# A normalisation's sums over four channel groups: one instruction with a single input in place of a chain of additions

## The chip, the core and the metric

The kernel runs on one core of one Trainium2 chip. The core's engines run side by side and wait for one another through semaphores: TensorE (PE in the profile, its weight loads PEld) multiplies matrices into PSUM, VectorE (DVE) and GpSimd (POOL) do elementwise work and sums along a partition, ScalarE (ACT) does functions of one input, and SyncE (SP) issues most DMAs. Data lie in SBUF, 128 partitions wide; matmul results lie in PSUM, which DVE and ACT can read. The metric is the device time of one execution in microseconds; the kernel's time is the median of its runs.

## What is computed

Eight batches of 576 positions with 512 channels, in float32. Linear attention in eight heads gives x; a gated convolution mixer gives a second x; then a Fourier mixing, a normalisation over the channels and a two-layer network with a residual:

```python
X = np.fft.fft(np.fft.fft(x, axis=1), axis=2)
u = x + np.real(X).astype(np.float32)
mu = np.mean(u, axis=-1, keepdims=True)
var = np.mean((u - mu) ** 2, axis=-1, keepdims=True)
un = (u - mu) / np.sqrt(var + 1e-06)
out = u + np.maximum(un @ w_ch1, 0.0) @ w_ch2        # 512 -> 2048 -> 512
```

The change concerns the two means over the 512 channels.

## The kernel before

The kernel has four stages: attention with the conversion of the weights (to about 360 us of the span), the mixer and the Fourier transforms of batches 0 to 5 (to about 600 us), the last two batches together with the normalisation of the first block (to about 655 us), and the two-layer network (the rest).

The network works on nine blocks of 512 positions (`TB`; `NBK` = 9 of them), each as two halves of 256 columns (`HB`). The channels lie on partitions: 512 channels are four groups of 128, so a block's activations are the tile `A`, 128 partitions x 4 groups x 512 columns. There are two passes over the blocks (`blocks`): the first with one half of the hidden units, blocks 0 to 8 upwards; the second with the other half, blocks 8 to 0 downwards. The first pass normalises each block and stores it to DRAM (`un_scr`); the second loads the stored blocks again. Products are done in three matmuls with operands split into a high and a low part (`o_hi` on ACT, `o_lo` on DVE or POOL), and a block's 2 x 2 products are replaced by seven (`prep_un` makes the seven left operands `un`, `c1_units` the first layer with its ReLU and the operands `h` of the second, `c2_units` the second layer, whose results are added into four accumulators `acc`). Each of a block's two groups of hidden units takes fourteen such products, of twelve matmuls each.

`ln_stages` is the normalisation of one block. For each half it adds the four channel groups of `A` into `s1` (three additions of 256 columns), splits `s1` into `sh` and `sl` and has PE sum over the partitions with a matrix of 1/512 (two matmuls into `mean`). DVE subtracts `mean` from `A`. ACT squares `A` into the tiles `T0` (groups 0 and 1) and `T1` (groups 2 and 3), and three more additions of 256 columns add these four groups into `s1`. Again `sh`, `sl` and a matmul; ACT takes the root, DVE the reciprocal (two of 128 columns a half) and multiplies `A` by it. `T0` and `T1` serve `prep_un` afterwards.

The order of all this is not written out. Each step is noted in `ops` with the engines that may do it, a time for each, and the tiles that it reads and writes. `place_ops` then takes one step after the other: each engine gets, among the steps that are ready, the one due first, and a step with two engines to choose from (`"vp"`: DVE or POOL) goes to POOL if POOL would have it done before DVE. The additions are such steps (`e1` is `"vp"`), as are the `sl`, `un`, `h` and differences of `c`. The planner's times for a step are `COST`, and 0.87 us for a reciprocal; they know nothing of one engine holding up another. Tiles named `wo` and `wg` in rows below are spare parts of weight tiles that serve as `h`. All instructions of one helper carry one line: L647 is every `o_tt`, L72 a low part on DVE, L75 one on POOL, L66 a high part, L650 every `o_act`, L806 a product of the first layer, L875 one of the second, L721 and L722 the means.

Of the kernel before, what the change touches and what calls it, by code (L numbers as in the profile page):

```python
# [7 lines left out]
F32 = mybir.dt.float32  # L8
# [4 lines left out]
ALU = mybir.AluOpType  # L13
AX = mybir.AxisListType
# [10 lines left out]
HB = TB // 2  # L25
# [9 lines left out]
def attention_moe_mixer_kernel(  # L35
# [18 lines left out]
    nc = tc.nc  # L54
    mm = nc.tensor.matmul

    def pool(stack, name, bufs, space=None, side=None):
        kw = {} if space is None else {"space": space}
        if side is not None:
            kw["side"] = side  # L60
        if space is not DRAM:
            kw["reuse_waits"] = "tile"
        return stack.enter_context(tc.tile_pool(name=name, bufs=bufs, **kw))
# [521 lines left out]
    tl = {}  # L585
    ops = []

    def w_tiles(p, i, j):
        return [[p.tile([128, 7, 128], F32R, name=f"w{i}_{j}_{o}_{k}") for k in range(2)] for o in range(2)]

    def w_views(t):
        return [t[:, 896 * k:896 * k + 896].rearrange("p (q f) -> p q f", f=128) for k in range(2)]

    def open_mlp():
        p = pool(lx, "lx", 1, side=R)
        P["pss"] = pool(lx, "pss", 1, PSUM, side=R)
        wt[0].append(w_tiles(p, 0, 0))
        tl["s1"] = p.tile([128, TB], F32, name="s1")
        tl["A"] = p.tile([128, 4, TB], F32, name="A")
        for n in ("sh", "sl"):  # L600
            tl[n] = p.tile([128, HB], F32R, name=n)
        for i in range(2):
            tl["T", i] = p.tile([128, 2, HB], F32, name=f"T{i}")
            wr.append(p.tile([128, 7, 128], F32, name=f"wr{i}"))
        tl["mean"] = P["pss"].tile([128, HB], F32, name="mean")
        for i in range(7):
            un_op.append([p.tile([128, 2, HB], F32R, name=f"un{i}_{k}") for k in range(2)])
        wt[0].append(w_tiles(p, 0, 1))
        g = [P["g1"].tile([128, 2304], F32R, tag=f"g{i}", name=f"wg{i}") for i in range(2)]
        wt[0].append([w_views(t) for t in g])  # L610
        wt[0].append([w_views(wo_all[:, i]) for i in range(2)])
        h_more.extend(t[:, 1792:2304].rearrange("p (o f) -> p o f", f=HB) for t in g)
        h_more.append(wo_all[:, :, 1792:2048])
# [19 lines left out]
    def op(e, cols, fn, reads, writes, dur=None, more=0.0):  # L633
        if dur is None:
            dur = {k: COST[k][0] + COST[k][1] * cols / 1000 for k in e}
        else:
            dur = {e: dur}
        ops.append((dur, fn, reads, writes, more))

    def o_hi(dst, src, cols, r, w):  # L640
        op("a", cols, lambda e: hi_act(dst, src), r, w)

    def o_lo(e, dst, src, hi, cols, r, w):
        op(e, cols, lambda e: (lo_dve if e == "v" else lo_pool)(dst, src, hi), r, w)

    def o_tt(e, o, x, y, alu, cols, r, w):
        op(e, cols, lambda e: (nc.vector if e == "v" else nc.gpsimd).tensor_tensor(out=o, in0=x, in1=y, op=alu), r, w)  # L647

    def o_act(o, x, func, cols, r, w, **kw):
        op("a", cols, lambda e: nc.scalar.activation(out=o, in_=x, func=func, **kw), r, w)  # L650
# [57 lines left out]
    def ln_stages(t, e1=K["ln"]):  # L708
        a, s1 = tl["A"], tl["s1"]
        halves = [slice(0, HB), slice(HB, TB)]  # L710

        def add(o, x, y, e, r, w):
            o_tt(e, o, x, y, ALU.add, HB, r, w)

        def mean(k):
            sh, sl, p = tl["sh"], tl["sl"], tl["mean"]
            o_hi(sh, s1[:, halves[k]], HB, [("s1", k)], ["sh"])
            o_lo(e1, sl, s1[:, halves[k]], sh, HB, [("s1", k), "sh"], ["sl"])

            def f(e):  # L720
                mm(p, ones, sh, start=True, stop=False)  # L721
                mm(p, ones, sl, start=False, stop=True)  # L722
            op("m", 0, f, ["sh", "sl"], ["mean"], 0.218)
            return p

        for k, hk in enumerate(halves):
            for c in range(1, 4):
                add(s1[:, hk], s1[:, hk] if c > 1 else a[:, 0, hk], a[:, c, hk], e1,
                    [("A", c // 2, k), ("A", 0, k), ("s1", k)], [("s1", k)])
        for k, hk in enumerate(halves):  # L730
            p = mean(k)
            for c in range(2):
                b = a[:, 2 * c:2 * c + 2, hk]
                o_tt("v", b, b, p.unsqueeze(1).to_broadcast([128, 2, HB]), ALU.subtract, 2 * HB,
                     ["mean", ("A", c, k)], [("A", c, k)])
        for k, hk in enumerate(halves):
            for c in range(2):
                q = tl["T", c]
                o_act(q, a[:, 2 * c:2 * c + 2, hk], ACTF.Square, 2 * HB, [("A", c, k)], [("T", c)])
                if c:  # L740
                    add(s1[:, hk], s1[:, hk], q[:, 0], e1, [("s1", k), ("T", c)], [("s1", k)])
                    add(s1[:, hk], s1[:, hk], q[:, 1], e1, [("s1", k), ("T", c)], [("s1", k)])
                else:
                    add(s1[:, hk], q[:, 0], q[:, 1], e1, [("T", c)], [("s1", k)])
        for k, hk in enumerate(halves):
            p = mean(k)
            o_act(s1[:, hk], p, ACTF.Sqrt, HB, ["mean"], [("s1", k)], bias=eps)
        for k, hk in enumerate(halves):
            for z in range(2):
                x = s1[:, k * HB + z * 128:k * HB + z * 128 + 128]  # L750
                op("v", 0, lambda e, x=x: nc.vector.reciprocal(out=x, in_=x), [("s1", k)], [("s1", k)], 0.87)  # L751
            for c in range(2):
                b = a[:, 2 * c:2 * c + 2, hk]
                o_tt("v", b, b, s1[:, hk].unsqueeze(1).to_broadcast([128, 2, HB]), ALU.mult, 2 * HB,
                     [("s1", k), ("A", c, k)], [("A", c, k)])
        if t:
            store_un(t)

    def store_un(t):
        o_dma([(un_scr[t], tl["A"])], AK, [("un_scr", t)], 1024, K["sq"] if t == 0 else "d")  # L760
# [240 lines left out]
    def run_last(b):  # L1001
        ps = [P["ps"].tile([128, 512], F32, tag="ps", name=f"ps{i}") for i in range(4)]
        ps += [P["ps2"].tile([128, 512], F32, tag="ps2", name=f"ps{i}") for i in (4, 5)]
        ring = ((("ps", i % 6), ps[i % 6]) for i in range(1000))
        tl["fs"] = P["fs"].tile([128, 2, NE], F32, tag="fs", name="fs")
        tl["eo"] = P["x2"].tile([128, 2, 4, NE], F32, tag="eo", name="eo")
        tl["u"] = P["x2"].tile([128, 4, S], F32, tag="u", name="u")
        tl["u256"] = P["x2"].tile([97, S], F32, tag="u256", name="u256")
        y = [P["x2"].tile([128, 2, 2, NL], F32R, tag=f"Y{i}", name="Y") for i in range(2)]
        xb = P["x2b"].tile([128, 4, 2, NE], F32, tag="x2", name="x2")  # L1010
        f = fhl[b]
        load_a(0, u_scr)
        drain(prep_w(0, 0, K["w0"]))
        drain(prep_w(0, 1, K["w0"]))
        ln_stages(0, K["ln0"])
        note_FD(b, f, y, ring)
        note_W(b + 1, geo[b + 1], xb, f, ring)
        note_SD(b, x2[b], y, ring)
        if K["wl"]:
            drain(prep_w(0, 2, K["w"]))  # L1020
        note_FD(b + 1, f, y, ring)
        note_SD(b + 1, xb, y, ring)
        prep_un(0, K["un0"])
        op("m", 0, lambda e: None, [("un", i, k) for i in range(7) for k in range(2)]
           + [("w", 0, j, o, k) for j in range(2) for o in range(2) for k in range(2)], [], 0.0)
        with tc.manual_schedule():
            for i, e in place_ops():
                ops[i][1](e)
        ops.clear()
# [339 lines left out]
```

## Time and profile before

| | us |
|---|---|
| median of 3 runs (1435.16 to 1440.01) | 1435.16 |
| the profiled execution | 1437.34 |
| its span in the profile | 1435.5 |
| from 677 to 1022 us: first pass of the network | 345 |
| one block of the first pass, 890.45 to 934.52 | 44.07 |
| one block of the second pass, 1105 to 1145 | 40.00 |

The profile page gives busy time by engine; further views of the same trace give it by stretch, or list the instructions of one engine in order of time, each with its start, its duration and, in brackets, how long the engine was idle before and what ended that. An instruction's duration may overlap the next one's by some 0.08 us on DVE, so a step on a busy engine is read from one start to the next. A duration includes the time in which an instruction that had started could not go on. The chain of waits follows the work that ended last backwards; its pieces do not overlap, and "issue" in it is time in which the engine waited for nothing that the profile shows.

### The profile page before, as it was taken

The numbers are of one execution on the slowest core, as the hardware profiler recorded it, in microseconds if no ns is written. First come the engines' busy times: TensorE is split into PE (matmuls) and PEld (weight loads), VectorE is DVE, ScalarE is ACT, GpSimd is POOL, SyncE is SP. The second block draws the span as 40 slices with busy tenths as digits, with TensorE's granted clock in tenths as the row PEclk, the third lists the DMA queues.
The fourth block names the chain that finished last, engine by engine and source line by source line (L and its number), as shares of the span: only waits on it lengthen the run. The fifth ranks groups of instructions, "written<-read, shape, count | busy, mean of one in ns | idle before, by whom it ended". The sixth has DMA issues, their size and how long they took to land.

```text
span 1435.5 us, 35040 instructions
## 1 busy us (share of the span) xinstructions
PE 1347.1 (94%) x14672; PEld 1297.1 (90%) x14672; DVE 1242.7 (87%) x1938; ACT 814.7 (57%) x1513; POOL 706.0 (49%) x526
## 2 busy tenths in 40 slices
PE   6899999997999999986899899999999999999998
PEld 6788888886999999976799899999999999999998
DVE  6689989876899999797999999999899887788876
ACT  5778888764545545464555554555465555444442
POOL 3858887732667666563555555545425111111111
PEclk9899999999999999998999999999999999999999
DMA  6347777741334433336323232222332222222211
GB/s 244 137 182 256 273 266 278 245 169 41 133 133 144 144 134 107 109 109 212 121 82 118 90 111 82 96 97 89 123 124 97 89 74 78 71 89 89 89 40 50
DMA packets 89851, 186.98 MB, mean 130 GB/s; under 512 B 10455, under 2 KB 37335, under 8 KB 87518
## 3 DMA queue, kind: packets, MB, share of 16 engines
q1 hardware_dynamic: 88488, 181.33, 37.2%
q10 hardware_dynamic: 1206, 3.41, 0.6%
q8 instruction: 115, 1.88, 0.5%
q14 instruction: 42, 0.34, 0.1%
HBM read 121.79 MB, written 62.93 MB: 129 GB/s over the span
## 4 chain that ended last, share of the span: by engine, by line
PE 43%; DVE 30%; POOL 9%; issue 8%; ACT 5%; DMA 4%; SPq 0%; ACTq 0%; DVEq 0%; POOLq 0%
PE cx L875 9%; PE x L806 9%; PE cy L875 5%; PE y L806 4%; DVE acc L424 4%; DVE A L647 3%; DVE c L647 3%; PE z L806 3%; PE kv L243 2%; DVE acc L647 2%; PE cz L875 2%; DMA raw<-in_w_ch_dram 2%; DVE s L751 2%; PE nm L282 2%; PE pj L204 2%
## 5 line engine op out<-in xcount | busy, mean ns | idle before, releaser
L875 PE MATMUL cx<-h,w 128*128 128x256 f32 x1152 | 176.2, 286 | 4.8 <-ACT h L66 2.5
L875 PEld LDWEIGHTS cx<-h,w 128*128 128x128 f32 x1152 | 158.3, 194 | 6.7 <-ACT h L66 3.1
L66 ACT ACTIVATE h<-c 128x512 fp32r<-128x512 f32 x180 | 111.6, 627 | 38.6 <-DVE c L647 22.2
L647 POOL TENSOR_TENSOR c<-c,c 128x512 f32<-128x512 f32 x35 | 49.7, 1421 | 167.9 <-ACT h L650 128.2
L647 DVE TENSOR_TENSOR acc<-cx,acc 128x512 f32<-128x512 f32 x144 | 98.1, 681 | 32.9 <-PE cx L875 32.2
L650 ACT ACTIVATE c<-c 128x512 f32<-128x512 f32 x108 | 67.9, 630 | 100.6 <-DVE c L647 99.3
L806 PE MATMUL x<-un,w 128*128 128x256 f32 x864 | 117.0, 285 | 7.6 <-DVE eo L647 6.9
L875 PE MATMUL cy<-h,w 128*128 128x256 f32 x864 | 117.3, 284 | 4.6 <-DVE h L72 1.9
L75 POOL TENSOR_TENSOR h<-c,h 128x512 fp32r<-128x512 f32 x33 | 48.1, 1459 | 148.9 <-ACT h L66 148.7
L806 PEld LDWEIGHTS x<-un,w 128*128 128x128 f32 x864 | 109.9, 193 | 8.2 <-issue 7.1
L424 DVE SCALAR_TENSOR_TENSOR acc<-xf,cw,acc 128x576 f32<-128x576 f32 x128 | 105.0, 820 | 11.9 <-ACT acc L422 10.6
L875 PEld LDWEIGHTS cy<-h,w 128*128 128x128 f32 x864 | 108.9, 191 | 7.0 <-DVE h L72 2.5
L243 PE MATMUL kv<-vraw,ke 128*64 128x66 f32 x2560 | 97.6, 230 | 14.6 <-ACT ke L222 9.8
L243 PEld LDWEIGHTS kv<-vraw,ke 128*64 128x64 f32 x2560 | 85.1, 141 | 26.2 <-ACT ke L222 13.2
L72 DVE TENSOR_TENSOR h<-c,h 128x512 fp32r<-128x512 f32 x111 | 104.2, 940 | 1.3 <-ACT h L66 0.7
L211 DVE TENSOR_REDUCE m<-pj 128x8 f32<-128x1024 f32 (+1 forms) x80 | 88.7, 1108 | 10.6 <-PE pj L204 10.6
L204 PE MATMUL pj<-wp,kqraw 64*128 64x128 f32 x1152 | 89.4, 294 | 5.7 <-DMA kqraw<-in_k_dram 4.9
L204 PEld LDWEIGHTS pj<-wp,kqraw 64*128 64x128 f32 x1152 | 73.8, 194 | 19.6 <-issue 18.1
L214 DVE TENSOR_TENSOR y<-pj,m 128x1024 f32<-128x1024 f32 (+1 forms) x80 | 88.7, 1109 | 0.4
L282 PE MATMUL nm<-kvT,qe 128*64 128x65 f32 x2304 | 84.4, 225 | 2.8 <-issue 1.3
L75 POOL TENSOR_TENSOR ge<-gs,ge 128x580 fp32r<-128x580 f32 x32 | 46.7, 1460 | 76.1 <-ACT ge L66 76.1
L99 POOL TENSOR_SCALAR mt<-mt 128x1024 f32<-128x1024 f32 (+1 forms) x21 | 55.6, 2650 | 57.4 <-DVE mt L97 47.3
(249 smaller groups left out, 4222.4 us busy)
## 6 DMA issues: line engine op xcount, KB each, us to landing
raw<-in_w_ch_dram SPq DMA_DIRECT2D x16, 1024.0 KB, 8.2
wr<-w_scr SPq DMA_DIRECT2D x32, 448.0 KB, 3.4
vraw<-in_v_dram SPq DMA_DIRECT2D x16, 660.0 KB, 9.3
x_scr<-xT SPq DMA_DIRECT2D x32, 288.0 KB, 6.5
xf<-x_scr SPq DMA_DIRECT2D x8, 1152.0 KB, 5.9
out_dram<-acc SPq DMA_DIRECT2D x36, 256.0 KB, 2.2
kqraw<-in_k_dram SPq DMA_DIRECT2D x15, 576.0 KB, 8.3
kqraw<-in_q_dram SPq DMA_DIRECT2D x15, 576.0 KB, 7.4
```

What stands on the lines that cost most here:

```text
L66: nc.scalar.activation(out=dst, in_=src, func=ACTF.Copy)
L72: nc.vector.tensor_tensor(out=dst, in0=src, in1=f32(hi), op=ALU.subtract)
L75: nc.gpsimd.tensor_tensor(out=dst, in0=src, in1=f32(hi), op=ALU.subtract)
L204: mm(p[:, h, o:o + F], t[r, w, 128 * c:128 * c + 128], wp[r, :], start=True, stop=True)
L211: nc.vector.tensor_reduce(out=m, in_=pv, axis=AX.X, op=ALU.max, apply_absolute_value=True)
L214: nc.vector.tensor_tensor(out=y, in0=pv, in1=m.unsqueeze(3).to_broadcast([128, 2, 2 * n, F]), op=ALU.subtract)
L243: mm(t[p, w, :], e[:, a, h, j, p], tv[:, h, slot, :], start=slot % 5 == 0 and w == 0, stop=slot % 5 == 4 and w == 3, skip_group_check=True)
L282: mm(t[p, 2 * j + h, 0:65], e[:, a, h, j, p], kt[:, 2 * h + a, b, :], start=(a == 0), stop=(a == 1))
L424: nc.vector.scalar_tensor_tensor(out=acc, in0=shifted(t), scalar=cw[:, m, t:t + 1], in1=acc, op0=ALU.mult, op1=ALU.add)
L647: op(e, cols, lambda e: (nc.vector if e == "v" else nc.gpsimd).tensor_tensor(out=o, in0=x, in1=y, op=alu), r, w)
L806: mm(p[:, n], l, v[:, kt], start=first and n + kt + m == 0, stop=kt == 1 and m == 2, skip_group_check=True)
L875: mm(p[:, o], v, r[:, n], start=first and o + n + m == 0, stop=n + m == 3, skip_group_check=True)
```

## The change

Each chain of three additions becomes one `tensor_reduce` on DVE: it reads a view of the four channel groups with the group as the innermost index, so four elements that are 512 columns (2 KB, in `A`) or 256 columns (1 KB, in `T`) apart, adds them and writes one. For the second sum the two tiles `T0` and `T1` become the halves of one tile `T`. The steps no longer have POOL to choose; the planner counts 1.1 us for each.

```diff
+        tl["T"] = p.tile([128, 2, 2, HB], F32, name="T")
         for i in range(2):
-            tl["T", i] = p.tile([128, 2, HB], F32, name=f"T{i}")
+            tl["T", i] = tl["T"][:, i]
...
-        def add(o, x, y, e, r, w):
-            o_tt(e, o, x, y, ALU.add, HB, r, w)
-
...
+        def total(k, v, r):
+            o = s1[:, halves[k]]
+            op("v", 0, lambda e: nc.vector.tensor_reduce(out=o, in_=v, axis=AX.X, op=ALU.add), r, [("s1", k)], 1.1)
+
         for k, hk in enumerate(halves):
-            for c in range(1, 4):
-                add(s1[:, hk], s1[:, hk] if c > 1 else a[:, 0, hk], a[:, c, hk], e1,
-                    [("A", c // 2, k), ("A", 0, k), ("s1", k)], [("s1", k)])
+            total(k, a[:, :, hk].rearrange("p c s -> p s c"), [("A", 0, k), ("A", 1, k)])
...
             for c in range(2):
                 q = tl["T", c]
                 o_act(q, a[:, 2 * c:2 * c + 2, hk], ACTF.Square, 2 * HB, [("A", c, k)], [("T", c)])
-                if c:
-                    add(s1[:, hk], s1[:, hk], q[:, 0], e1, [("s1", k), ("T", c)], [("s1", k)])
-                    add(s1[:, hk], s1[:, hk], q[:, 1], e1, [("s1", k), ("T", c)], [("s1", k)])
-                else:
-                    add(s1[:, hk], q[:, 0], q[:, 1], e1, [("T", c)], [("s1", k)])
+            total(k, tl["T"].rearrange("p c o s -> p s (c o)"), [("T", 0), ("T", 1)])
```

Since the planner places every step anew, the order changes around the sums too. On DVE, in a block in the middle of the first pass, the rows from the mean's subtraction to the last sum of squares stood like this before (`s_9173` is `s1`, `T_9177` and `T_9179` are `T0` and `T1`, `c` and `h` belong to the first layer, `acc` to the second):

```order
L647 TENSOR_TENSOR A<-A,mean 128x2x256 x2
L647 TENSOR_TENSOR c_9638<-y,c_9638 128x512
L647 TENSOR_TENSOR s_9173<-T_9177 128x256
L647 TENSOR_TENSOR acc_9679<-cx,acc_9679 128x512
L647 TENSOR_TENSOR c_9637<-c_9638,c_9637 128x512
L647 TENSOR_TENSOR A<-A,mean 128x2x256 x2
L850 SCALAR_TENSOR_TENSOR h_1_9659<-x_9643,h_0_9658 128x512
L647 TENSOR_TENSOR s_9173<-T_9177 128x256
L72 TENSOR_TENSOR h_1_9653<-c_9637,h_0_9652 128x512
L647 TENSOR_TENSOR s_9173<-s_9173,T_9179 128x256
L647 TENSOR_TENSOR c_9639<-c_9639,c_9637 128x512
L647 TENSOR_TENSOR s_9173<-s_9173,T_9179 128x256
```

With the change the same stretch of DVE, from the sums of `A` on, is this:

```order
L726 TENSOR_REDUCE s_9173<-A 128x256 x2
L72 TENSOR_TENSOR sl<-s_9173,sh 128x256
L648 TENSOR_TENSOR c_9630<-x_9634,c_9630 128x512
L648 TENSOR_TENSOR acc_9671<-cx,acc_9671 128x512
L648 TENSOR_TENSOR acc_9669<-cy,acc_9669 128x512
L648 TENSOR_TENSOR A<-A,mean 128x2x256 x2
L72 TENSOR_TENSOR sl<-s_9173,sh 128x256
L648 TENSOR_TENSOR acc_9670<-cx,acc_9670 128x512
L726 TENSOR_REDUCE s_9173<-T 128x256
L648 TENSOR_TENSOR A<-A,mean 128x2x256 x2
L648 TENSOR_TENSOR c_9629<-y,c_9629 128x512
L846 SCALAR_TENSOR_TENSOR h_1_9646<-x_9634,h_0_9645 128x512
```

One more reduction of `T` stands right behind it. The chain of adds between rows of `h` and `c` is gone, and the differences of `c` and one `h` have left this stretch for POOL. POOL had this before, in the rows from the first layer's last `h` to the low part of the second mean:

```order
L75 TENSOR_TENSOR wo<-c_9638,h_0_9660 128x2x256
L647 TENSOR_TENSOR s_9173<-A 128x256
L647 TENSOR_TENSOR s_9173<-s_9173,A 128x256
L75 TENSOR_TENSOR h_1_9651<-c_9637,h_0_9650 128x512
L75 TENSOR_TENSOR sl<-s_9173,sh 128x256
L647 TENSOR_TENSOR s_9173<-s_9173,T_9179 128x256 x2
L647 TENSOR_TENSOR c_9638<-c_9639,c_9638 128x512
L75 TENSOR_TENSOR sl<-s_9173,sh 128x256
```

With the change POOL has this there:

```order
L75 TENSOR_TENSOR wo<-c_9629,h_0_9651 128x2x256
L75 TENSOR_TENSOR un_1_9188<-T,un_0_9187 128x512
L75 TENSOR_TENSOR h_1_9642<-c_9628,h_0_9641 128x512
L75 TENSOR_TENSOR h_1_9648<-c_9630,h_0_9647 128x512
L75 TENSOR_TENSOR sl<-s_9173,sh 128x256
L648 TENSOR_TENSOR c_9628<-c_9629,c_9628 128x512
L648 TENSOR_TENSOR c_9629<-c_9630,c_9629 128x512
```

POOL's four adds of a block and two of its three `sl` are gone; it has one more each of `h`, of the first and of the second step of `T` in `prep_un`, two more differences of `c`, and one less each of `un` and `wo`. On DVE a block has eight adds less and four reductions more, two `sl`, one `un` and one `wo` more, and one step of each kind of `T`, two differences of `c` and one `h` less.

## Rows read from the trace of the kernel before

**Rows 1.** The page: busy us of each engine, share of the span, instructions.
```profile
PE 1347.1 (94%) x14672; PEld 1297.1 (90%) x14672; DVE 1242.7 (87%) x1938; ACT 814.7 (57%) x1513; POOL 706.0 (49%) x526
```

**Rows 2.** Stretch, length; busy PE, PEld, DVE, ACT, POOL (x instructions); clock, DMA share, GB/s.
```profile
604.00:677.00 73.00, 54.95 (x378) 52.07 (x376) 62.63 (x94) 42.16 (x84) 35.32 (x21) 0.91 0.49 166
677.00:1022.00 345.00, 323.18 (x2589) 315.91 (x2590) 334.00 (x474) 184.03 (x332) 193.88 (x146) 0.99 0.30 97
```

**Rows 3.** The same view, one block of each pass.
```profile
890.45:934.52 44.07, 42.34 (x344) 41.36 (x345) 42.65 (x62) 23.68 (x44) 23.90 (x19) 1.00 0.29 96
1105.00:1145.00 40.00, 40.00 (x337) 40.00 (x337) 34.28 (x50) 19.83 (x34) 7.31 (x6) 1.00 0.25 80
```

**Rows 4.** Chain of waits in that block: start, length, what.
```profile
899.31 0.13 PE mean L722
...
933.87 0.61 DVE h L72
...
934.52 1.57 PE cx L875 x11
```

**Rows 5.** DVE's timeline there: start, duration, line, operation, tiles, sizes, idle before.
```profile
904.84 0.42 DVE L647 TENSOR_TENSOR s<-T 128x256 f32<-128x256 f32 x1
905.18 1.23 DVE L72 TENSOR_TENSOR h<-c,h 128x512 fp32r<-128x512 f32 x1
906.33 1.51 DVE L647 TENSOR_TENSOR s<-s,T 128x256 f32<-128x256 f32 x1
...
909.30 0.94 DVE L751 RECIPROCAL s<-s 128x128 f32<-128x128 f32 x1
910.16 0.62 DVE L72 TENSOR_TENSOR h<-c,h 128x512 fp32r<-128x512 f32 x1
...
922.11 0.68 DVE L72 TENSOR_TENSOR un<-T,un 128x512 fp32r<-128x512 f32 x1
922.71 0.68 DVE L72 TENSOR_TENSOR h<-c,h 128x512 fp32r<-128x512 f32 x1
```

**Rows 6.** POOL's timeline in the same block.
```profile
904.94 0.92 POOL L75 TENSOR_TENSOR sl<-s,sh 128x256 fp32r<-128x256 f32 x1
905.82 1.74 POOL L75 TENSOR_TENSOR wo<-c,h 128x512 fp32r<-128x512 f32 x1
909.45 0.74 POOL L75 TENSOR_TENSOR sl<-s,sh 128x256 fp32r<-128x256 f32 x1 [1.90 <-ACT sh L66]
914.33 1.29 POOL L75 TENSOR_TENSOR wg<-c,wg 128x512 fp32r<-128x512 f32 x1 [4.14 <-ACT wg L66]
```

**Rows 7.** One-input rows in the attention stage: DVE's timeline.
```profile
100.33 1.22 DVE L211 TENSOR_REDUCE m<-pj 128x8 f32<-128x1024 f32 x1
101.46 0.15 DVE L291 TENSOR_SCALAR r<-nm 128x4 f32<-128x4 f32 x1
...
103.33 0.69 DVE L94 TENSOR_SCALAR cv<-raw 128x1024 int32<-128x1024 int32 x1
103.93 0.69 DVE L211 TENSOR_REDUCE m<-pj 128x4 f32<-128x512 f32 x1
```

**Rows 8.** One-input rows of DVE and POOL by shape: count, busy us, mean ns, idle.
```profile
L211 DVE TENSOR_REDUCE m<-pj 128x8 f32<-128x1024 f32 x64 | 77.8, 1215 | 10.6 <-PE pj L204 10.6
L211 DVE TENSOR_REDUCE m<-pj 128x4 f32<-128x512 f32 x16 | 10.9, 682 | 0.0
L99 POOL TENSOR_SCALAR mt<-mt 128x1024 f32<-128x1024 f32 x20 | 55.4, 2770 | 57.4 <-DVE mt L97 47.3 <-ACT ke L222 10.2
```

**Rows 9.** The tile T, ACT's squares: ns shortest/median/longest.
```profile
L650 ACT ACTIVATE T<-A x36: 614/632/637, 617.4 to 992.7; 128x512 f32<-128x512 f32 x36
```

## The prediction

> **What bounds the kernel now.** The page's head and busy shares come first [rows 1]: PE is busy 94% of the span and DVE 87%, but these are means over stages, so the next view is the busy time by stage [rows 2]. The reader is to see three stages there in which the normalisation runs or ends. From 604 to 677 us (the end of the last Fourier batches, and block 0's normalisation) PE is busy 54.95 of 73 us and DVE 62.63. From 677 to 1022 us (the first MLP pass, blocks 0 to 8, with the normalisation of blocks 1 to 8 inside) DVE is busy 334.00 of 345 us, or 97%. From 1105 us on there is no normalisation; there PE has work all the time. One stretch of each kind of each kind [rows 3] makes it exact: a block of the second pass is 40.00 us for 337 matmuls with PE busy throughout, so 344 matmuls (a block of the first pass, with the eight of the means) are worth 344 x 40.00 / 337 = 40.8 us. The block from 890.45 to 934.52 takes 44.07 us, and DVE is busy 42.65 of them. So in the first pass DVE sets the period, and up to 3.2 us a block lie between it and PE's own time. The chain of waits says the same [rows 4]: from the mean's matmul at 899.31 it stays on DVE until 933.87, with pieces called issue in between, and then returns to PE at 934.52.
>
> Why is DVE busy so long? One block is 61 DVE instructions (the 62 of [rows 3] count one that began before its edge); their timeline, of which [rows 5] has seven, gives 48 of 512 columns, 9 of 256 (8 of them the adds of the sums) and 4 reciprocals. From one start to the next they take 0.60, 0.34 and 0.86 us where nothing disturbs them (922.11 to 922.71, 904.84 to 905.18, 909.30 to 910.16) [rows 5]. That is 28.8 + 3.1 + 3.4 = 35.3 us. The other 42.65 - 35.3 = 7.35 us are **blocked time**: the add at 906.33 took 1.51 us where its kind takes 0.42, and the h row before it 1.23 where 0.68 is usual [rows 5], while POOL's sl (904.94) and wo (905.82) ran [rows 6]. wo itself was drawn out to 1.74 from 1.29 [rows 6]. Both blocked DVE rows read two SBUF tiles. The reciprocal at 909.30, with one SBUF input, ran its usual 0.94 us across POOL's sl of 909.45, and sl its usual 0.74 [rows 5, 6]: those two did not hold each other. So I count DVE instructions with two SBUF inputs (21 of 512 columns and the 9 of 256, 15.7 us, 44% of 35.3) as those that POOL can block. POOL's work in a block is 12 instructions of 512 columns at 1.29 and 7 of 256 at 0.74 us, 20.7 us undisturbed [rows 6]; each microsecond of it cost DVE 7.35 / 20.7 = 0.356 us.
>
> **The change part by part**, for one steady block (in the order six blocks of the first pass hold the same 56 DVE and 16 POOL instructions).
>
> The adds. Eight DVE adds leave: 8 x 0.34 = 2.7 us. Four POOL adds leave: 4 x 0.74 = 3.0 us.
>
> The four reductions. Each reads 1024 elements and writes 256. Before has no reduction from SBUF and none that steps 1 or 2 KB between elements. The nearest row is the same operation over 1024 elements in PSUM: 1.13 us from start to start (100.33 to 101.46) [rows 7], 1.04 ns for each further element ((1215 - 682) / 512) [rows 8]. The price's lower end is the one-input row L94, which steps over every second word and passes 1024 in 0.60 us (103.33 to 103.93) [rows 7]; the upper end is POOL's one-input row over 1024 elements, 2.77 us [rows 8]. I take 1.13, since operation and count are the same: 4 x 1.13 = 4.5 us on DVE.
>
> What the planner moves. It no longer counts POOL for the sums, and gives POOL other work. By the order DVE loses a net three instructions of 512 columns (-1.8 us) and gains two of 256 (+0.7); POOL gains three (+3.9) and loses two (-1.5). The sum for DVE is 35.3 - 2.7 + 4.5 - 1.8 + 0.7 = 36.0 us, 0.7 more than before; for POOL 20.1, 0.6 less.
>
> Blocked time. This is where the gain must come from. Of DVE's 36.0 us only 18 instructions of 512 columns and 3 of 256 still have two SBUF inputs: 11.8 us, 33%. If POOL's work meets them as often as their share says, it costs 0.356 x 33/44.4 x 20.1 = 5.3 us in place of 7.35. DVE is then busy 41.3 us; with the 1.42 us it was idle before (44.07 - 42.65) the period is 42.7 us, 1.37 us less. PE's 40.8 us lie below that, so DVE still sets the period.
>
> Times 7.5 blocks (2589 matmuls between 677 and 1022 us [rows 2], 344 a block): -10.3 us.
>
> From 604 to 677 us. DVE is the chain there too. Block 0's eleven DVE adds (11 x 0.34 = 3.7 us) become four reductions (4.5 us): +0.8 us. The one POOL add that goes had its sum waiting for it, but I count nothing for that.
>
> The wait that is added. A reduction of squares waits for both Square instructions of its half, and the next half's Squares wait for it, since it frees all of T; before, T's first half was free after one add. Behind it on DVE's queue stand the subtraction of the mean and an accumulation, whose PSUM tile PE needs. The planner knows this wait and puts an accumulation ahead of the reduction; while DVE has other work to take, it costs nothing, and if that cover is gone it costs a Square (0.63 us [rows 9]) and a reduction (1.13 us) a block.
>
> Sum: -10.3 + 0.8 = -9.5 us. The profiled execution took 1437.34 us (span 1435.5), so it would become 1427.8; the median of the runs is 1435.16, 2.2 us below it, and **1425.7, so 1426 us**, is the forecast for that.
>
> [...]
>
> **The rivals.**
> 1. *The reads are slow.* Each element of a reduction lies 1 or 2 KB from the one before it, and a read that cannot follow at one element a step would draw out all four. For it: nothing in the trace reads like that, and L211's elements lie side by side. Against it: L94's step of two words costs nothing [rows 7]. The price if each element takes two steps: 1.13 + 1.07 = 2.2 us. DVE's undisturbed sum is 40.2 us, blocked time 0.356 x 29/44.4 x 20.1 = 4.7, the period 46.4: +2.3 us x 7.5, and 4 x 1.07 + 0.8 from 604 to 677, or +22.5 us: 1458 us. It decides from a reduction of 1.53 us on (the period is 44.07 again).
> 2. *The blocked time stays.* What POOL takes over is 512 columns wide where the adds were 256, and all of it reads SBUF; the planner knows nothing of blocking. If each microsecond of POOL costs DVE 0.356 us as before, the blocked time is 7.2 us and the period 44.6: +0.5 x 7.5 + 0.8 = +5 us, 1440 us. For it: of the rows drawn out before, most are 512 wide. Against it: DVE has 4.5 us a block more in which POOL can run freely.
> 3. *The added wait shows.* Half of 1.76 us exposed a block takes back 6.6 of the 9.5 us: 1432 us. Against it: idle time on DVE is 1.42 us a block now, and DVE has a queue of other rows.
>
> **How the numbers follow.** Forecast 0.45, rival 1 0.37, rival 2 0.11, rival 3 0.07. The forecast's own range is 1415 to 1437 (blocked time may fall nearly to what PE allows, or not at all). Rival 1 spreads from 1440 (1.6 us) past 1458 (2.2 us); the upper end, 2.77 us, gives some 1475. The range 1415 to 1458 leaves out the slowest third of rival 1 and little of the rest. This kernel's measurement tells 0.5%, or 7 us, from no change. Two thirds of the forecast's chance lie beyond that, and little of rival 3: faster 0.32. All but a few hundredths of rival 1 are slower, and a little of rival 2: slower 0.37. The rest, 0.31, is the same.
>
> **What would show it.** The mean of a reduction's row: 1.2 us recorded (1.13 and the overlap of 0.08) for the forecast, 1.6 or more for rival 1. The period of a block between 850 and 980 us: 42.7, 46.4, 44.6, 43.6. DVE's busy time in a block: 41.3 us, and if it is below 40 with a period above 42.7, a wait took its place. Adds drawn out to 1.5 us must be gone; whether h, un and c rows are drawn out as often tells rival 2. The forecast is wrong at once if a reduction next to a POOL row is drawn out, since then one SBUF input is no protection.

## The result

| | before | with the change |
|---|---|---|
| median of the runs beside each other | 1435.53 us (1435.16 to 1440.01) | 1454.41 us (1446.78 to 1459.56) |
| profiled execution (its span) | 1437.34 us (1435.5) | 1459.56 us (1457.7) |

The ratio is 1.0111, with a 95% interval of 1.0085 to 1.0138: the kernel is 1.1% slower, 19 us, where 9.5 us less was forecast.

In the page of the kernel with the change, the line that answers to [rows 1], DVE has 51 instructions less than before and is busy 26.5 us longer; POOL is busy 8.6 us less:

```profile
PE 1358.4 (93%) x14672; PEld 1303.8 (89%) x14672; DVE 1269.2 (87%) x1887; ACT 817.0 (56%) x1513; POOL 697.4 (48%) x505
```

The main cause, as the experiments below bear out, stands in the view of the tile `s` (shortest, median and longest ns of one instruction, first and last start):

```profile
L726 DVE TENSOR_REDUCE s<-A x18: 1937/2024/2070, 616.5 to 1006.5; 128x256 f32<-128x1024 f32 x18
L726 DVE TENSOR_REDUCE s<-T x18: 1971/2007/2043, 625.5 to 1017.3; 128x256 f32<-128x1024 f32 x18
```

A reduction takes 2.02 us recorded. The forecast had 1.2 us recorded and 1.13 from start to start. All 36 lie within 7% of one another.

On balance the extra time lies in seven blocks of the first pass. In both kernels SP stores the last part of block 0 (`part_scr`), and 7 blocks later that of block 7; the busy time by stage between these two stores, in the columns of [rows 2], is for the kernel before

```profile
724.89:1035.13 310.24, 295.26 (x2398) 289.39 (x2398) 297.44 (x426) 164.94 (x299) 171.69 (x130) 0.99 0.29 96
```

and with the change this, with one block of it that answers to the first line of [rows 3]:

```profile
731.38:1057.26 325.88, 303.30 (x2428) 293.01 (x2429) 319.95 (x395) 169.15 (x303) 163.34 (x110) 1.00 0.28 92
...
892.32:938.78 46.46, 43.05 (x346) 41.55 (x344) 45.84 (x57) 24.02 (x43) 23.76 (x17) 1.00 0.28 92
```

310.24 us became 325.88, 15.6 us more; DVE's busy time grew by 22.5 us and its idle time fell from 12.8 to 5.9. From that store to the end both kernels take 400.4 us, and from the load of block 0's `A` (SP's issue at 604.80, now 611.33) to the first of the two stores 120.09 and 120.05. The other 6.5 us of the two profiled spans lie ahead of that load, where both kernels have the same instructions; nothing of the change acts there. The medians differ by 18.9 us, 3.3 more than the seven blocks show, and the four runs with the change lie 12.8 us apart.

In one block, DVE's timeline (columns as in [rows 5]) shows what fills it:

```profile
899.83 1.81 DVE L72 TENSOR_TENSOR un<-T,un 128x512 fp32r<-128x512 f32 x1
901.56 1.78 DVE L648 TENSOR_TENSOR c<-c,c 128x512 f32<-128x512 f32 x1
...
911.63 3.99 DVE L726 TENSOR_REDUCE s<-A 128x256 f32<-128x1024 f32 x2
...
924.38 2.01 DVE L726 TENSOR_REDUCE s<-T 128x256 f32<-128x1024 f32 x1
...
935.29 3.46 DVE L648 TENSOR_TENSOR A<-A,s 128x512 f32<-128x512 f32 x3
```

and POOL's timeline (columns as in [rows 6]) shows what it did beside these:

```profile
899.80 2.99 POOL L75 TENSOR_TENSOR h<-c,h 128x512 fp32r<-128x512 f32 x2
...
913.13 1.30 POOL L75 TENSOR_TENSOR h<-c,h 128x512 fp32r<-128x512 f32 x1 [5.76 <-ACT h L66]
...
924.67 2.67 POOL L648 TENSOR_TENSOR c<-c,c 128x512 f32<-128x512 f32 x2 [1.27 <-ACT c L651]
```

The reductions at 911.63 and 924.38 have POOL's `h` and `c` running beside them; neither side is drawn out (POOL's usual time is 1.29 us [rows 6]; the `h` takes 1.30, and the two `c`, from 924.67 to 927.34, 1.29 and 1.30). The `un` and `c` at 899.83 and 901.56 still are, 1.8 us where 0.68 is usual, beside POOL's two `h` of 899.80. The chain of waits (start, length, what; answering to [rows 4]) has the reductions on it:

```profile
911.03 0.69 DVE c L648
911.72 3.63 DVE s L726 x2
...
924.38 0.58 DVE s L726
```

### The profile page after: what moved, and what is told of

The parts are those of the page before. It is cut to its first block, busy times and chain, and to the rows that moved or that the text cites. A ratio compares the mean times of both kernels' runs of the same rounds, so it can differ in the third digit from the quotient of the medians.

```text
span 1457.7 us, 34975 instructions
## 1 busy us (share of the span) xinstructions
PE 1358.4 (93%) x14672; PEld 1303.8 (89%) x14672; DVE 1269.2 (87%) x1887; ACT 817.0 (56%) x1513; POOL 697.4 (48%) x505
## 4 chain that ended last, share of the span: by engine, by line
PE 41%; DVE 34%; POOL 7%; issue 6%; ACT 6%; DMA 5%; SPq 0%; DVEq 0%; POOLq 0%; ACTq 0%
PE cx L871 9%; PE x L802 8%; PE cy L871 4%; PE y L802 4%; DVE acc L424 4%; DVE A L648 3%; DVE acc L648 3%; DVE s L726 3%; PE kv L243 3%; DVE c L648 3%; PE z L802 3%; PE pj L204 2%; DMA raw<-in_w_ch_dram 2%; DVE un L72 2%; PE nm L282 2%
## 5 line engine op out<-in xcount | busy, mean ns | idle before, releaser
L75 POOL TENSOR_TENSOR h<-c,h 128x512 fp32r<-128x512 f32 x44 | 62.5, 1428 | 198.4 <-ACT h L66 198.4
L648 POOL TENSOR_TENSOR c<-c,c 128x512 f32<-128x512 f32 x42 | 59.7, 1421 | 175.5 <-ACT h L651 126.6
L72 DVE TENSOR_TENSOR h<-c,h 128x512 fp32r<-128x512 f32 x100 | 95.3, 953 | 2.6 <-ACT h L66 2.0
L75 POOL TENSOR_TENSOR ge<-gs,ge 128x580 fp32r<-128x580 f32 x32 | 46.7, 1460 | 79.0 <-ACT ge L66 79.0
```

Source lines behind the costliest of these rows:

```text
L72: nc.vector.tensor_tensor(out=dst, in0=src, in1=f32(hi), op=ALU.subtract)
L75: nc.gpsimd.tensor_tensor(out=dst, in0=src, in1=f32(hi), op=ALU.subtract)
```

## The experiments

The theories. **A, the reading step**: a reduction is slow because its elements lie 1 or 2 KB apart. **B, the order**: the planner's new order, with its new choice of engine for the other steps, costs or hides time by itself. **C, blocking**: the blocked time did not fall as forecast, whatever the reduction costs. Each measured ratio is to the kernel before on the same chip, with its 95% interval.

For eight of the kernels the following table gives one block in the middle of the first pass (from one store of `un_scr` to the next). "Drawn out" is worked out row by row from DVE's timeline: what each row took beyond 0.68 us for 512 columns (0.60 for each further one in a joined row) or 0.42 for 256, where that is over 0.1 us. Its three parts are the sums with their neighbours; the un, T, c and h rows between two normalisations; and the last step `A<-A,s`.

| kernel | period | DVE busy | drawn out | at the sums | un, T, c, h | A<-A,s |
|---|---|---|---|---|---|---|
| before | 44.07 | 42.65 | 7.1 | 2.0 | 3.4 | 1.7 |
| the change | 46.46 | 45.84 | 6.6 | 0.25 | 4.8 | 1.6 |
| e1_adjacent | 45.00 | 43.23 | 6.8 | 0.65 | 4.8 | 1.3 |
| e9_old_order | 46.79 | 45.49 | 5.1 | 0 | 3.4 | 1.7 |
| e9b_old_adjacent | 43.51 | 42.21 | 5.1 | 0 | 3.4 | 1.7 |
| e10_old_order_dve | 43.99 | 43.00 | 6.3 | 1.2 | 3.4 | 1.7 |
| e3_adds_dve | 47.24 | 45.16 | 10.3 | 4.5 | 4.8 | 1.0 |
| e12_lat | 44.13 | 41.59 | 6.6 | 2.3 | 3.4 | 0.9 |

### e1_adjacent: the changed kernel, reading four adjacent elements

```diff
-            o = s1[:, halves[k]]
+            o = s1[:, halves[k]].rearrange("p (c s) -> p c s", c=4)
...
-            total(k, a[:, :, hk].rearrange("p c s -> p s c"), [("A", 0, k), ("A", 1, k)])
+            total(k, a[:, :, hk].rearrange("p c (s f) -> p c s f", f=4), [("A", 0, k), ("A", 1, k)])
...
-            total(k, tl["T"].rearrange("p c o s -> p s (c o)"), [("T", 0), ("T", 1)])
+            total(k, tl["T"].rearrange("p c o (s f) -> p (c o) s f", f=4), [("T", 0), ("T", 1)])
```

> The four reductions of a block read four neighbouring columns of one channel group in place of four columns 1 or 2 KB apart; count, sizes and the rest of the notes to the planner are as in the change. The means are of other numbers, so this kernel computes something else. Step theory (the reductions are slow because each element lies far from the last): a reduction's row falls from 2.01 us recorded to 1.2, DVE's undisturbed sum in a block to 36.0 us, and with 5.3 to 6.6 us blocked and 0.6 to 1.4 us idle a block takes 42 to 44 us and the kernel 1420 to 1437 us. Group theory (a reduction that writes an element after every four is slow, or one that reads SBUF, wherever they lie): the row stays at 2.0 us, the block at 46.5 and the kernel near 1454.

In this kernel the means are of other numbers; only its time is of use. Measured: 1439.85 us beside 1437.94, ratio 1.0014 (1.0003 to 1.0025). The tile `s` and two reductions in a row on DVE's timeline:

```profile
L726 DVE TENSOR_REDUCE s<-A x18: 1206/1208/1220, 610.9 to 986.9; 128x256 f32<-128x1024 f32 x18
```

```profile
895.84 2.33 DVE L726 TENSOR_REDUCE s<-A 128x256 f32<-128x1024 f32 x2
```

and one block in the columns of [rows 2]:

```profile
876.52:921.52 45.00, 42.14 (x346) 41.33 (x345) 43.23 (x57) 24.08 (x43) 23.77 (x17) 1.00 0.29 95
```

From start to start a reduction takes 2.33 - 1.21 = 1.12 us here, the price of the forecast, and 3.99 - 2.02 = 1.97 in the changed kernel. Nothing else differs in the instructions or their order, so in this order theory A carries nearly all of the slowdown: the kernel falls from 1.1% above before to 0.1%. But the block is 45.00 us where the forecast had 42.7 for this very price. That is C, and 6.8 us of drawn-out rows against 5.3 forecast show it.

### e5_steps: four steps in one kernel

```diff
+                v2, o2 = a[:, 0:2, :].rearrange("p c s -> p s c"), s1
...
+                v8, o8 = a[:, :, hk].rearrange("p c (s f t) -> p c s t f", f=4, t=2), s1[:, hk].rearrange("p (c s t) -> p c s t", c=4, t=2)
...
+                vp = tl["T"].rearrange("p c o (s t) -> p s (c o) t", t=2)
...
+                v16, o16 = tl["T"].rearrange("p c o (f s) -> p (c o) s f", f=4), s1[:, hk].rearrange("p (c s) -> p c s", c=4)
```

> The reductions' price by their steps, one view each in a block: (1) two groups 2 KB apart, alternating, 1024 elements to 512; (2) groups of four elements at a step of two words, 256 elements to 64, four times; (3) pairs of neighbouring words, the pairs 1 KB apart, 1024 elements to 128; (4) groups of four elements 256 B apart, 1024 to 256. The sums are of other numbers than the normalisation's. Step theory: (4) is about 2.0 us like the change's reductions. If only the distance from one element to the next counts, (1) is 2.0 as well and (3) lies between 1.2 and 2.0, since half of its steps are long; (2) is 0.34 at the rate of one element in 1.04 ns. If a pair of neighbouring words is what the read wants, (3) is 1.2. [...]

Measured: 1443.18 us in one run, and in the view of the tile `s`:

```profile
L736 DVE TENSOR_REDUCE s<-A x36: 397/410/426, 616.0 to 991.6; 128x64 f32<-128x256 f32 x36
...
L750 DVE TENSOR_REDUCE s<-T x18: 1206/1210/1220, 624.3 to 993.7; 128x128 f32<-128x1024 f32 x18
...
L732 DVE TENSOR_REDUCE s<-A x9: 1247/1252/1261, 614.7 to 985.8; 128x512 f32<-128x1024 f32 x9
L753 DVE TENSOR_REDUCE s<-T x9: 1973/2032/2046, 631.0 to 998.4; 128x256 f32<-128x1024 f32 x9
```

L736 steps over every second word: 0.41 us for 256 elements, as fast as an add of 256 columns (0.42 before). L750 reads two adjacent words and then hops 1 KB: 1.21 us, as in e1 with all elements adjacent. L732 alternates between two places 2 KB apart: 1.25 us, 3% more than adjacent. L753 takes its four elements from places only 256 bytes apart, and with 2.03 us is as slow as the change's 1 and 2 KB (2.01 and 2.02). So from 256 bytes to 2 KB it is not the length of the hop: two places in turn cost 0.04 us for 1024 elements, four cost 0.8. Four words that lie 8 bytes apart (L736) show no such cost: by estimate, e1's 1.21 us less 768 elements at the 1.04 ns of [rows 8] is 0.41 too. Where it turns, between two places and four and between 8 bytes and 256, was not tried. This kernel's sums, too, are of other numbers.

### e3_adds_dve and e10_old_order_dve: the adds stay, all on DVE

The first tells the planner that all adds are DVE's, so that it orders anew; the second keeps the order of before, and only emits each add on DVE.

```diff
-            o_tt(e, o, x, y, ALU.add, HB, r, w)
+            o_tt("v", o, x, y, ALU.add, HB, r, w)
```

> The kernel before, but the additions may no longer go to POOL; POOL takes other work as the planner sees fit. It does what the change does to the engine without the reduction. If the loss comes from the sums being bound to DVE, this kernel loses too: twelve adds at 0.34 us are 4.1 us of DVE a block, against 2.7 before, and a block takes 45 us or more, the kernel 6 us more or worse. If it comes from the price of the reductions (4 x 1.93 = 7.7 us), this kernel stays within 4 us of before.

```diff
-            o_tt(e, o, x, y, ALU.add, HB, r, w)
+            op(e, HB, lambda _: nc.vector.tensor_tensor(out=o, in0=x, in1=y, op=ALU.add), r, w)
```

> The order of the kernel before, with the additions that went to POOL issued on DVE at the same place among the others. Binding theory (the loss of the kernel with adds on DVE alone, 3.2 us a block, comes from the adds being there): four adds more on DVE and four less on POOL a block give 36.7 us undisturbed and, since every add can be blocked, 10 us blocked: 47 us a block, about 20 us slower than before. Order theory (that loss came from the new order around them): 36.7 + 6.3 blocked + 1.4 idle = 44.4 us a block, within 6 us of before.

Measured: 1458.42 us, 1.0140 (1.0119 to 1.0162), with the new order; 1439.62 beside 1437.71, 1.0007 (0.9985 to 1.0030), with the old. The same adds on the same engine, 19 us apart: that is B, alone. The first adds of the squares show the blocking that the change was to avoid, in e3

```profile
L647 DVE TENSOR_TENSOR s<-T x18: 410/1491/1526, 617.4 to 1013.8; 128x256 f32<-128x256 f32 x18
```

and in e10

```profile
L713 DVE TENSOR_TENSOR s<-T x18: 407/414/1514, 617.8 to 993.5; 128x256 f32<-128x256 f32 x18
```

Their medians are 1.49 and 0.41 us. In e3's order POOL has h and c rows beside the sums, as it has in the change's order; there a reduction beside two c of POOL keeps its 2.01 us (924.38 in the change), and the adds beside POOL's h take 1.53 and 1.49 (914.10 and 919.32 in e3).

### e9_old_order and e9b_old_adjacent: reductions in the order of before

The planner sees the same three adds with their engines as before; the first two emit nothing, and the third emits the reduction. e9 reads as the change does, e9b adjacent elements, so that e9b's means are of other numbers. The diff shown is e9's.

```diff
-                add(s1[:, hk], s1[:, hk] if c > 1 else a[:, 0, hk], a[:, c, hk], e1,
+                add(red(s1[:, hk], a[:, :, hk].rearrange("p c s -> p s c")) if c == 3 else none, e1,
...
-                    add(s1[:, hk], s1[:, hk], q[:, 0], e1, [("s1", k), ("T", c)], [("s1", k)])
-                    add(s1[:, hk], s1[:, hk], q[:, 1], e1, [("s1", k), ("T", c)], [("s1", k)])
+                    add(none, e1, [("s1", k), ("T", c)], [("s1", k)])
+                    add(red(s1[:, hk], tl["T"].rearrange("p c o s -> p s (c o)")), e1, [("s1", k), ("T", c)], [("s1", k)])
```

> The changed kernel's reductions in the order of the kernel before: the planner still places twelve additions a block and everything else as before, but of each chain of three only the last place is filled, by a reduction on DVE; the other two places stay empty. Every other instruction keeps its engine and its place. Price theory (the loss is what the reductions take on DVE): four at 1.94 us in place of 8 DVE adds at 0.34 make DVE's undisturbed sum 40.3 us a block, 17.7 us of POOL at 0.33 to 0.36 us blocked add 5.8 to 6.4, idle time 0.6 to 1.4: 46.7 to 48.1 us a block, 18 to 28 us more than before. Order theory (most of the loss comes from the planner's new order): a block takes 45.3 us or less and the kernel is less than 9 us slower than before.

> As the one with the reductions in the order of before, but they read four neighbouring columns (so the sums are of other numbers). Price theory: four at 1.13 make DVE's sum 37.1 us a block, 5.8 to 6.4 blocked, 0.6 to 1.4 idle, 43.5 to 44.9 us: between 4 us faster and 6 us slower than before. The difference to the same with far steps is the steps' price alone: 4 x 0.81 = 3.2 us a block if nothing takes it up, 23 us; the planner's own order with and without far steps differed by 1.46 us a block. If single-input reductions free DVE from POOL as the prediction had it, the blocked time here is 4.7 us or less.

Measured: e9 1461.64 us, 1.0192 (1.0155 to 1.0230); e9b 1432.63, 0.9976 (0.9960 to 0.9992), both beside 1437.71. The same block of e9, and then of e9b, in the columns of [rows 2]:

```profile
890.85:937.64 46.79, 43.49 (x346) 41.65 (x345) 45.49 (x58) 23.79 (x43) 20.66 (x15) 1.00 0.28 91
```

```profile
875.81:919.32 43.51, 42.10 (x347) 41.32 (x346) 42.21 (x58) 23.91 (x43) 20.48 (x15) 1.00 0.30 98
```

46.79 - 43.51 = 3.28 us a block, and DVE's busy time differs by the same 3.28: four reductions of 2.02 against 1.21 are 3.24. In this order the step of the read costs its price in full. And with it gone the reductions gain: e9b is 5 us below before, with sums that this kernel could not use.

The drawn-out rows of e9b are, from DVE's timeline of that block, these:

```profile
876.31 1.40 DVE L648 TENSOR_TENSOR T<-A 128x512 f32<-128x512 f32 x1
...
882.43 1.25 DVE L72 TENSOR_TENSOR un<-T,un 128x512 fp32r<-128x512 f32 x1
883.60 1.78 DVE L648 TENSOR_TENSOR c<-c,c 128x512 f32<-128x512 f32 x1
...
887.11 1.17 DVE L648 TENSOR_TENSOR c<-c,c 128x512 f32<-128x512 f32 x1
...
888.81 1.19 DVE L72 TENSOR_TENSOR un<-T,un 128x512 fp32r<-128x512 f32 x1
...
915.12 4.17 DVE L648 TENSOR_TENSOR A<-A,s 128x512 f32<-128x512 f32 x4
```

The kernel before has the same six; the row of `A` shown here closes the block ahead of the other five:

```profile
914.90 4.16 DVE L647 TENSOR_TENSOR A<-A,s 128x512 f32<-128x512 f32 x4
919.59 1.40 DVE L647 TENSOR_TENSOR T<-A 128x512 f32<-128x512 f32 x1
...
925.71 1.25 DVE L72 TENSOR_TENSOR un<-T,un 128x512 fp32r<-128x512 f32 x1
926.87 1.78 DVE L647 TENSOR_TENSOR c<-c,c 128x512 f32<-128x512 f32 x1
...
930.38 1.18 DVE L647 TENSOR_TENSOR c<-c,c 128x512 f32<-128x512 f32 x1
...
932.08 1.18 DVE L72 TENSOR_TENSOR un<-T,un 128x512 fp32r<-128x512 f32 x1
```

They make 5.1 us in before, in e9, in e9b and in e10, to 0.02 us. Only the other 2.0 us of before's 7.1 lie at the sums: 1.24 in two adds, 0.55 in an h and 0.24 in a c. This is what C comes to.

### e2_plan_193: the planner is told the true price

```diff
-            op("v", 0, lambda e: nc.vector.tensor_reduce(out=o, in_=v, axis=AX.X, op=ALU.add), r, [("s1", k)], 1.1)
+            op("v", 0, lambda e: nc.vector.tensor_reduce(out=o, in_=v, axis=AX.X, op=ALU.add), r, [("s1", k)], 1.93)
```

> The changed kernel, but the planner counts a reduction at 1.93 us, the measured step from one to the next, and not at 1.1. If part of the loss is an order made for reductions that end sooner than they do, a block comes down from 46.46 us by 0.5 us or more, since more of the other work then goes to POOL, and the kernel gains 4 us or more on the change. If the loss is DVE's sum alone, the period stays within 0.3 us and the kernel within 3 us of the change.

Measured: 1452.84 us, 1.0103 (1.0066 to 1.0140). A block became 45.71 us, 0.75 less than the change's, so a part of the block's loss of 2.39 us came with the wrong number in the plan; 1.64 us of it stay with the true one. In the total nothing of that can be told: the ratio of the change was 1.0111. The wrong number was not the main cause.

### e4_first_only: only the sums of A become reductions

```diff
-                add(s1[:, hk], s1[:, hk] if c > 1 else a[:, 0, hk], a[:, c, hk], e1,
-                    [("A", c // 2, k), ("A", 0, k), ("s1", k)], [("s1", k)])
+            op("v", 0, lambda e, o=o, x=x: nc.vector.tensor_reduce(out=o, in_=x, axis=AX.X, op=ALU.add),
+               [("A", 0, k), ("A", 1, k)], [("s1", k)], 1.1)
```

> Only the sums of A are reductions; the sums of squares are the chains of before, with POOL to choose and with two tiles T0 and T1. If the loss is DVE's sum of times (two reductions of 1.93 in place of about 4 DVE adds and 2 POOL adds a block), a block takes 45.0 to 45.6 us and the kernel is 7 to 11 us slower than before. If the loss lies in the wait that the reduction of T adds (all four groups of squares before one sum, one tile T), this kernel is no slower than before by more than 2 us.

Measured: 1453.13 us, 1.0100 (1.0072 to 1.0129). Half the reductions cost as much as all of them, and both expectations were missed. They take the same 2.01 us each, so half the price left the kernel and something else took its place: in two of its blocks (837.39 to 930.65 us) the drawn-out rows come to some 7.8 us a block, by the busy time of each kind of row there, where the change has 6.6. An edit cannot be halved here without a new order.

### e12_lat: another order, the work of before

```diff
-    K = dict(hlo="vp", ht="vp", un="vp", ln="vp", w="vp", lat=0.2, lnat=6, bw=0.0028,
+    K = dict(hlo="vp", ht="vp", un="vp", ln="vp", w="vp", lat=0.25, lnat=6, bw=0.0028,
```

> The kernel before with one number of the planner changed: the delay that it counts from a step to the next one that needs it is 0.25 us and not 0.2. No instruction is added or taken away; only engines and places differ. If the order decides as much as the instructions, a block moves away from 44.07 us by 1 us or more and the kernel by 7 us or more. If DVE's sum decides, both stay within 0.4 us and 3 us.

Measured: 1443.88 us, 1.0046 (1.0025 to 1.0066): 6.2 us from one number of the planner, with every instruction of the kernel before. The steady block did not move (44.13 us in the table, where 1 us or more was expected of the order theory); where the 6.2 us lie was not followed up.

### e7_squares_pe and e8_both_pe: the sums go to PE

To beat both kernels, the ones matrix was given each of the four groups in turn, rounded by ACT, instead of their sum: in e7 the squares, in e8 also the first sum (the low parts `sl` are left out there).

```diff
+            for c in range(4):
+                n = ("sh", "sl")[c % 2]
+                o_act(tl[n], a[:, c, halves[k]], func, HB, [("A", c // 2, k)], [n])
+                op("m", 0, lambda e, c=c, n=n: mm(p, ones, tl[n], start=c == 0, stop=c == 3),
+                   [n] + (["mean"] if c else []), ["mean"], 0.109)
```

> The kernel before, but the sums of squares leave DVE and POOL: ACT squares each channel group of 256 columns into a tile that PE reads, and four matmuls add the groups and the partitions at once, in place of three adds, a high and a low part and two matmuls a half. PE gets four matmuls of 0.12 us a block more, DVE and POOL lose six adds and two low parts. If DVE's sum sets the period, about 2 us of undisturbed DVE time and 2 us of POOL's go, a block takes 41.5 to 42.8 us, and the kernel is 8 to 17 us faster than before. If the period is held by something else (the wait from mean to mean), it stays within 3 us. The squares are rounded to the matmul's high part.

> As the one with the squares on PE, and the first sums too: ACT copies each group's high part for PE, so no adds and no low parts of sums are left. Against that one DVE loses another 2 to 3 us a block, and ACT gains some 0.8. If DVE's sum still set the period, a block falls to PE's own time, 352 matmuls or 41.8 us, and the kernel is 12 to 20 us faster than before; if PE sets it already there, it is no faster than the one with the squares alone. The mean is then of values rounded to their high part.

Measured: e7 1435.39 us beside 1440.02, 0.9981 (0.9957 to 1.0005); e8 1446.61, 1.0045 (1.0029 to 1.0060). One block of e7, and four of e8:

```profile
841.45:886.65 45.20, 42.75 (x351) 41.86 (x350) 41.99 (x60) 23.49 (x45) 17.48 (x13) 1.00 0.29 94
```

```profile
800.88:987.62 186.74, 174.99 (x1399) 171.03 (x1398) 160.00 (x231) 103.66 (x203) 37.46 (x26) 0.98 0.30 95
```

DVE is busy 0.7 us a block less than before in e7 and 2.7 less in e8 (160.00 / 4 = 40.0), yet the blocks are 45.2 and 46.7 us: DVE's idle time rose from 1.4 to 3.2 and 6.7 us. Neither gains the 8 us or more that were expected: e7 can't be told from before, though that block of it is longer, and e8 is slower. Which waits hold them was not followed up.

## Why the prediction was wrong

**The price of a reduction: wrong, and the step that turned the sign.** The forecast chose 1.13 us by "the same operation and count" over the upper rows; measured is 1.97. The row it went by reads elements that lie side by side, and that was the property that counted: with adjacent elements (e1) the step is 1.12. With the measured price its own sum (36.0 + 4 x 0.84 = 39.4) is what the block shows (45.84 busy less 6.6 drawn out, 39.2). Rival 1 named this, and its turning point of 1.53 us is passed. That its period, 46.4 us, is the measured 46.46 is partly luck: it had 2.2 us for a reduction where 1.97 was measured, 4.7 us of blocked time where the rows say 6.6, and 1.42 us of idle time where 0.62 was left. The sentence against it, that L94's step of two words is free, is true (L736 of e5, 0.41 us for 256 elements) and says nothing of four places 256 bytes or more apart.

**Blocked time: wrong, hidden behind the price.** The forecast scaled all 7.35 us by DVE's share of two-input work, down to 5.3. At the forecast's price (e1) the rows say 6.8, and by the prediction's own reckoning, busy less undisturbed, 43.23 - 36.0 = 7.2: rival 2's figure. So at its own price the forecast would have missed as well: it had 9.5 us less than before and rival 2 had 5 more; e1 is 1.9 us above the kernel before on its chip. But the reason is not a constant share of POOL's time: in e9b POOL has 17.7 us (before's 20.7 less four adds of 0.74), DVE 5.1 us of drawn-out rows, 0.29, where before's 7.1 of 20.7 are 0.34. The blocked time sits on particular rows. Two microseconds lay at the sums, and those the reductions took away as intended; the other 5.1 lay on rows that the change does not touch, and the new order made 6.4 of them (4.8 and 1.6). In it POOL's un, T, c and two h run without a pause from 894.64 to 902.79 beside DVE's rows; that this is the reason is likely, but no run tested it by itself.

**Undisturbed sums, idle time, the added wait: right.** DVE's sum with the price put right is 0.2 us off. DVE's idle time fell to 0.62 us a block (46.46 - 45.84), so the added wait (rival 3) does not show: what is slower covers it. At the forecast's price (e1) 1.77 us are idle, so at most the 0.35 us above before's 1.42 could be that wait.

**One input is protection: right.** Reductions keep their time beside POOL in every kernel (1.89 to 2.07 us over four places 256 bytes or more apart, 1.16 to 1.22 adjacent); two-input adds in the same place take 1.49 us (e3).

**How many blocks: off by a little. Block 0: zero on balance, from two errors.** Seven periods carry the difference, not 7.5 (15.6 / 7 = 2.2 us a block). Block 0's normalisation was forecast to cost 0.8 us, and by the measured price it is 4 x 1.97 - 3.7 = 4.2. From the load of its `A` to the first of the two stores, a stretch that holds block 1's normalisation too, the two kernels take the same, 120.09 and 120.05 us. But the strided reads are not free there: with adjacent reads the change's order takes 114.37 us (e1), and the order of before takes 118.35 with adjacent (e9b) and 123.31 with strided reads (e9). So they cost 5.7 and 5.0 us, and something else in the change gave as much back, which the forecast did not have; what it was stays open. That the term came out near 0.8 is luck. Each of these is one execution, and a part may be the granted clock of PE (in the mean of that stretch 0.86 with the change, where the kernel before had 0.91).

**The order, which had no term.** The prediction took the planner's moves as a count of instructions. At the same price of a read the new order costs 7.2 us with adjacent reads (1439.85 against 1432.63) and saves 7.2 with strided reads (1454.41 against 1461.64). In a block, the first is 1.49 us (45.00 against 43.51): 1.7 us more of drawn-out rows (6.8 against 5.1) and 0.5 more idle time, less 0.7 of undisturbed rows. The second is mostly cover: from e1 to the change the reductions grow by 3.2 us a block, but DVE's idle time falls from 1.77 to 0.62 and the period grows by only 1.46 (some 0.6 us of this are not accounted for), where from e9b to e9 nothing falls and it grows by 3.28. Why the planner's order leaves more idle time to be filled stays open. The two medians of each pair come from different chips, the kernels before beside them being 1437.94 and 1437.71, 1435.53 and 1437.71.

## What to carry to other kernels

Price a strided reduction by a row that strides the same way: how many places it visits in turn, and how far apart, counted here (1.21 us adjacent, 1.25 from two places, 2.0 from four), not only the operation and the count; where no row does, work out the slow end as a case of its own, as rival 1 did. Before counting on blocked time to go, list the drawn-out rows one by one and ask which of them the edit touches: here 2.0 of 7.1 us. And where a planner places every step anew, run the edit once in the old order, since the order alone moved this kernel by 6 to 19 us.

## What the runs showed of the hardware

- A DVE reduction over 1024 fp32 elements of SBUF takes 1.21 us when they are adjacent, or adjacent in pairs 1 KB apart (256 elements in every second word take 0.41); 1.25 us alternating between two places 2 KB apart; and 2.0 us cycling over four places, whether these are 256 bytes, 1 KB or 2 KB apart.
- No reduction from SBUF was held up by POOL's two-input rows in any run (the longest took 2.07 us over four places and 1.22 adjacent), and POOL's `h` and `c` of 512 columns that ran beside them in a block of the change took 1.29 and 1.30 us each. Adds of 256 columns with two SBUF inputs took 1.53 and 1.49 us beside POOL's h (914.10 and 919.32 in e3), where 0.41 is usual; the longest add in that kernel took 2.09.
